# Chunk bounds by eight concurrent tiles over two banks, with a fence, in a statically ordered attention kernel

## The chip, the cores and the metric

The kernel runs on one core of a Trainium2 chip. The metric is the device time of one execution, in microseconds (us). Before the change it is 231.66 us, the median of three runs (231.29 to 232.64). "Engines" are PE (the matmul engine), PEld (its weight loads, which overlap PE: in the profile of before they are busy for 129.5 us beside PE's 214.9 in a span of 230.5), DVE (the vector engine), ACT (the scalar engine), POOL (GpSimd) and SP (which issues most DMAs: 153 of the 167 that the profile of before lists).

## The reference, cut to what matters

Four batches, eight heads, 768 positions, head dimension 64. Keys come in 24 chunks of 32. For each query an upper bound of its score with each chunk picks the six best chunks; attention runs only over those. A gated feed-forward block (gMLP) follows.

```python
k_min = np.min(k_chunks, axis=3)
k_max = np.max(k_chunks, axis=3)
ub = np.sum(np.maximum(q[:, :, :, None, :] * k_min[:, :, None, :, :],
                       q[:, :, :, None, :] * k_max[:, :, None, :, :]), axis=-1)
ub = np.where(causal, ub, -1000000000.0)
top_chunks = np.argsort(ub, axis=-1)[..., -top_k:]      # top_k = 6
...                                                     # masked softmax attention
h = gelu(x @ w_in); u, v = h[..., :512], h[..., 512:]   # (written out in the original)
v_s = np.einsum('ts,bsd->btd', w_sg, v_n) + b_sg[None, :, None]
return x + (u * v_s) @ w_out
```

Since max(q·lo, q·hi) = q·lo + max(q, 0)·(hi − lo) for hi ≥ lo, the bound is a sum of two matrix products: `W[0]` (the minima) with q, and `W[1]` (maxima minus minima) with `rT` = max(q, 0).

## The kernel before

Heads are worked on in 16 pairs (two heads on 128 partitions: head one on 0–63, head two on 64–127), and a *select* finds the chunks of two pairs at once, so there are eight selects. Every piece of work is handed to a small list scheduler written into the kernel. It is given an assumed cost for each operation and an urgency for each kind of work (a table found earlier by a search over the scheduler's own model of the time), and it fixes, before anything runs, in what order each engine executes. The program gives every engine its list as one stream, with waits on semaphores in it; at one such wait in the changed kernel PE idled 3.32 us and ran nothing else meanwhile (the timeline is below).

```python
# key side of a pair: W[w][:,0] = minima, W[w][:,1] = maxima, then the difference in place
P.op("dve", lambda d: d.tensor_tensor(W[w][:, 1, 0:NC], W[w][:, 1, 0:NC], W[w][:, 0, 0:NC],
                                      op=ALU.subtract), 0.18, port=True, reads=ws, writes=ws)
...
# query side of a pair: both heads at once, 128 partitions x 576 columns
P.op("dve", lambda d: d.tensor_scalar(rT[w % 2][:], qT[w][:, LO:S], 0.0, None, op0=ALU.max),
     0.47, port=True, reads=qk, writes=[("rT", w % 2)])
...
def select(pairs):
    u = sel_of(pairs[0])
    for hf in range(2):                       # two halves of 288 queries, one PSUM bank each
        t = ps_g.tile(t_slots(pairs[0]))
        n = NSEL // 2
        def ub(e, t=t, hf=hf):
            for m in range(2):                # first W·q, then (difference)·max(q, 0)
                for j in (0, 2, 1, 3):        # four heads: four 64x32 tiles of the array
                    w, lo = pairs[j % len(pairs)] % 4, 64 * (j // 2)
                    rhs = qT[w][lo:lo + 64, ...] if m == 0 else rT[w % 2][lo:lo + 64, ...]
                    r = e.matmul(t.ap()[32 * j:32 * j + 32, 0:n], W[w][lo:lo + 64, m, :], rhs,
                                 start=(m == 0), stop=(m == 1), tile_position=(lo, 32 * j))
            return r
        P.op("pe", ub, 1.0, mode="ub", reads=..., writes=[t], alloc=t)
        P.op("dve", lambda d, ...: d.transpose(U[u]..., t.ap()[:, 0:n]), dve(n, "ps"), ...)
    ...                                       # MAX8, comparison, transpose: the mask Dt
```

The number after each function (0.18, 0.47, 1.0) is the cost that the scheduler assumes. `SIDE = 6` says that the scores of the first six pairs are computed by `scores` (two matmuls on 64 rows each, the mask added by further matmuls), those of the others by `scores_one` (full rows, with the mask sent into the operand's spare rows by small DMAs).

The softmax here doesn't subtract the row's maximum and nothing guards it: scores larger than these inputs give would overflow.

Of the kernel before, what the change touches and what calls it, by code (L numbers as in the profile page):

```python
# [13 lines left out]
LAT = {"pe": 0.15, "act": 0.25, "dve": 0.12, "pool": 0.15, "sp": 0.05}  # L14
# [36 lines left out]
class Program:  # L51
# [11 lines left out]
    def op(self, eng, fn, cost, reads=(), writes=(), ps=(), alloc=None, dma=None, table=None,  # L63
           burst=None, prio=None, lane=0, bulk=False, port=False, mode="full"):
        o = Op()
# [8 lines left out]
        ps = tuple(ps) + ((alloc,) if alloc is not None else ())  # L74
# [32 lines left out]
    def schedule(self):  # L107
# [3 lines left out]
        alloc = {o.alloc: o for o in ops if o.alloc is not None}  # L111
# [28 lines left out]
        def slot_for(t, now):  # L140
            best = None
            for i, own in enumerate(t.cls.owner):
                if t.slots is not None and i not in t.slots:
                    continue
                at = 0.0 if own is None else (own.end if own.left == 0 else None)
                if at is not None and (best is None or at < best[0]):
                    best = (at, i)
            return best

# [4 lines left out]
        while n < len(ops):  # L154
            pick = None
            for e in ENGINES:
                cands = []
                for i in ready[e]:
                    o = ops[i]
                    t = max(rt[i], free[e])  # L160
                    if o.alloc is not None and o.alloc.slot is None:
                        s = slot_for(o.alloc, t)
                        if s is None:
                            continue
                        t = max(t, s[0])
# [19 lines left out]
            if o.alloc is not None and o.alloc.slot is None:  # L185
                at, s = slot_for(o.alloc, t)
                old = o.alloc.cls.owner[s]
                if old is not None:
                    for x in old.users:
                        o.deps.setdefault(x, False)  # L190
                o.alloc.slot = s
                o.alloc.cls.owner[s] = o.alloc
                o.alloc.users = []
# [191 lines left out]
    "load": [-109, -94, 104, 570, 740, 1507, 425, 238, 1704, 1924, 1908, 1646, -23, 1323, 1316, 193],  # L385
    "k": [-173, 1463, 2123, 1531, 780, 272, 805, 1232, 858, 260, 499, 2021, 1327, 265, 1662, 1220],
    "q": [153, 446, 1733, 1884, -53, 768, 1388, 1712, 646, 352, 1619, 149, 1838, -64, 891, 1804],
    "loadv": [1232, 1270, 290, 178, 1412, 1731, 1539, 1414, 2195, 1824, 620, 120, 73, 2088, 414, 668],
    "v": [1246, 1773, 342, 1920, 1326, 645, -200, -63, 1450, 33, 50, 561, 714, 486, 422, 351],
    "sel": [470, 1537, 1414, 781, 346, 556, 2087, -51, 3, 2114, 490, 1502, 1878, 798, 1690, -200],  # L390
    "sc": [-200, 1272, -200, 17, 1196, 1646, 1679, -197, -28, 1484, -90, 4, 1572, 21, 24, 44],
    "pv": [1443, 370, 1445, 454, 78, 2144, 1213, 76, 721, 1663, 938, 638, -147, 176, 1396, 952],
    "xt": [443, 2013, 57, 514, 469, 383, 911, -30, 421, 1131, 124, 1380, 1215, 390, 258, 433],
    "wsg": [-182],
    "hv": [497, 543, -154, 490],
    "hu": [2065, 884, 201, 728],
    "pt": [-96, 2026, 372, 745, 1924, 1969, 1334, 596],
    "out": [1127, 1638, 1477, 1797, 2040, 1893, 1475, -31],
# [3 lines left out]
def dve(n, src="sb", rate=1.0):  # L402
    return ((120 if src == "ps" else 58) + n / rate) / 960.0 + 0.04


def act(n):
    return 0.12 + n / 1200.0
# [10 lines left out]
def _kernel(nc, q, k, v, w_in, g_ln, w_sg, b_sg, w_out, out):  # L418
# [13 lines left out]
    SIDE = 6  # L432
    XDMA = 1
    WDMA = 0
    FIRST = 0
    ROWB = ()
# [27 lines left out]
    with contextlib.ExitStack() as ctx:  # L464
        def T(name, shape, dt):
            return ctx.enter_context(nc.sbuf_tensor(name, list(shape), dt))

        P = Program()
        ps_score = PsumClass([ctx.enter_context(nc.psum_tensor(f"PSC{i}", [128, 1024], F32)) for i in range(2)])
# [12 lines left out]
        bsgbc = T("bsgbc", [128, S], F32) if len(ROWB) < B else None  # L482
        if ROWB:
            glnbc = T("glnbc", [128, F], F32)
            bsg3 = T("bsg3", [128, S], BF16)
            bsgf = T("bsgf", [1, S], F32)
            onesB = T("onesB", [128, 128], BF16)
            nmr = T("nmr", [128, NT], F32)

# [6 lines left out]
        W = [T(f"W{i}", [128, 2, 32], F32) for i in range(4)]  # L496
# [21 lines left out]
        vsT = [T(f"vsT{i}", [128, TG], F32) for i in range(2)] if len(ROWB) < B else None  # L518
# [42 lines left out]
        def weights(when):  # L561
            for after, i in when:
# [15 lines left out]
                else:  # L578
                    if len(ROWB) < B:
                        P.op("sp", lambda s: s.dma_start(bsgbc[:], bass.AP(b_sg.tensor, 0, [[0, 128], [1, S]])),  # L580
                             2.3, reads=after, writes=["bsgbc"], dma="bsg")
                        P.op("sp", gln_load, 0.3, reads=after, writes=["glnT"], dma="gln")
                    if ROWB:
                        P.op("sp", lambda s: s.dma_start(bsgf[:], bass.AP(b_sg.tensor, 0, [[S, 1], [1, S]])), 0.2,
                             reads=after, writes=["bsgf"], dma="bsgf")
                        P.op("sp", lambda s: s.dma_start(glnbc[:], bass.AP(g_ln.tensor, 0, [[0, 128], [1, F]])), 1.6,
                             reads=after, writes=["glnbc"], dma="glnbc")
                        at("wsg", 0)
                        P.op("pool", lambda g: g.memset(bsg3[:], 0.0), 0.5, reads=after, writes=["bsg3"])
                        P.op("pool", lambda g: g.memset(onesB[:], 1.0), 0.2, reads=after, writes=["onesB"])  # L590
                        for r in (0, 32, 64):
                            P.op("pool", lambda g, r=r: g.tensor_copy(bsg3[r:r + 1, :], bsgf[:]), 0.8, lane=r + 1,
                                 reads=["bsgf", "bsg3"], writes=["bsg3"])
                            if r < 64:
                                P.op("pool", lambda g, r=r: g.tensor_tensor(bsgf[:], bsgf[:], bsg3[r:r + 1, :],
                                                                            op=ALU.subtract), 1.2, lane=r + 1,
                                     reads=["bsgf", "bsg3"], writes=["bsgf"])
# [18 lines left out]
        def kside(p):  # L616
            s, w = p % NQS, p % 4
            for hf in range(2):
# [13 lines left out]
                for kt_, rows, key in ([(KA, slice(0, 128), "KA")] if p < SIDE else  # L632
# [5 lines left out]
            P.op("dve", lambda d: d.tensor_tensor(W[w][:, 1, 0:NC], W[w][:, 1, 0:NC], W[w][:, 0, 0:NC],  # L638
                                                  op=ALU.subtract), 0.18, port=True, reads=ws, writes=ws)
# [4 lines left out]
        def qside(p):  # L644
            s, w = p % NQS, p % 4
            for hf in range(2):
                t = ps_g.tile(t_slots(p))

                def tr(e, t=t, hf=hf):
# [10 lines left out]
            P.op("dve", lambda d: d.tensor_scalar(rT[w % 2][:], qT[w][:, LO:S], 0.0, None, op0=ALU.max),  # L660
                 0.47, port=True, reads=qk, writes=[("rT", w % 2)])
# [14 lines left out]
        def sel_of(p):  # L676
            return p % 2 if p < FIRST else (p // 2 + FIRST // 2) % 2

        def select(pairs):
            u = sel_of(pairs[0])  # L680
            for hf in range(2):
                t = ps_g.tile(t_slots(pairs[0]))
                n = NSEL // 2

                def ub(e, t=t, hf=hf):
                    for m in range(2):
                        for j in (0, 2, 1, 3):
                            w, lo = pairs[j % len(pairs)] % 4, 64 * (j // 2)
                            rhs = qT[w][lo:lo + 64, LO + n * hf:LO + n * hf + n] if m == 0 else \
                                rT[w % 2][lo:lo + 64, n * hf:n * hf + n]  # L690
                            r = e.matmul(t.ap()[32 * j:32 * j + 32, 0:n], W[w][lo:lo + 64, m, :], rhs,  # L691
                                         start=(m == 0), stop=(m == 1), tile_position=(lo, 32 * j))
                    return r
                ws = [p % 4 for p in pairs]
                P.op("pe", ub, 1.0, mode="ub",
                     reads=[("qT", w, h_) for w in ws for h_ in range(2)] + [("rT", w % 2) for w in ws] +
                     [("W", w, m, h_) for w in ws for m in range(2) for h_ in range(2)],
                     writes=[t], alloc=t)
                P.op("dve", lambda d, t=t, hf=hf: d.transpose(
                    U[u][:].rearrange("p b c -> p (b c)")[:, n * hf:n * hf + n], t.ap()[:, 0:n]),  # L700
                    dve(n, "ps"), reads=[t], writes=[("U", u, hf)], ps=[t])
            P.op("dve", lambda d: d.memset(U[u][:, 0, TOP + 1:TOP + 2], -3.0e38), 0.07,
                 writes=[("U", u, 0)])

            def m8s(d):
                for b in range(NBLK):
                    r = d.max(m8[u][:, b, :], U[u][:, b, 0:max(8, b + TOP + 1)])
                return r
            P.op("dve", m8s, 1.47, reads=[("U", u, 0), ("U", u, 1)], writes=[("m8", u)])
# [3 lines left out]
                 0.75, port=True, reads=[("U", u, 0), ("U", u, 1), ("m8", u)], writes=[("Dn", u)])  # L713
# [214 lines left out]
        def moe_g(b):  # L928
            s = b % 2
            for tg in range(2):  # L930
                at("pt", 2 * b + tg)
                for fb in range(NF):
                    t = ps_g.tile((2, 3))

                    def pt(e, t=t, fb=fb, tg=tg):
                        if b in ROWB:
                            e.matmul(t.ap()[:, 0:TG], onesB[:], bsg3[:, TG * tg:TG * tg + TG], start=True, stop=False)
# [138 lines left out]
```

## Time and profile before

| | before |
|---|---|
| time, median | 231.66 us |
| span of the profiled run | 230.5 us |
| PE busy, DVE busy | 214.9 us (93%), 185.3 us (80%) |
| one half of the bounds (eight tile matmuls twice) | 1.11 us |
| `rT` and W difference on DVE, all 16 pairs | 12.4 us |
| first gelu table load after the start-up (the first feed-forward block begins) | 54.3 us |

From the profile's page of before: busy time by engine, the granted PE clock in 40 slices of the span, and the share of each engine in the chain of waits (the chain that ended last).

```profile
PE 214.9 (93%) x2267; PEld 129.5 (56%) x2280; DVE 185.3 (80%) x532; ACT 158.1 (69%) x244; POOL 90.9 (39%) x117
PEclk9999799999999999999999999999999999999999
PE 76%; DVE 10%; ACT 9%; DMA 2%; issue 1%
```

PE is almost always busy and makes up three quarters of the chain. A saving on PE looks like a saving of time; DVE has a fifth of its time free.

Stretches of before: window and length, then for each engine its busy time and (number of instructions), the granted clock, DMA share, GB/s.

```profile
core 0: us, PE busy (x) PEld busy (x) DVE busy (x) ACT busy (x) POOL busy (x), PEclk, DMA share, GB/s
20.00:40.00 20.00, 17.18 (x249) 9.96 (x250) 13.42 (x43) 16.25 (x26) 11.55 (x15) 0.91 1.03 206
40.00:60.00 20.00, 17.96 (x260) 11.56 (x260) 14.83 (x37) 17.14 (x28) 11.89 (x18) 1.00 1.15 232
60.00:80.00 20.00, 19.99 (x192) 11.65 (x191) 18.88 (x72) 13.28 (x22) 9.65 (x10) 1.00 0.96 186
80.00:100.00 20.00, 19.95 (x278) 13.46 (x278) 16.26 (x53) 17.75 (x29) 11.17 (x14) 1.00 1.01 212
```

Until 60 us PE has gaps; in the stretches after it is nearly full.

The DVE groups by form (line, engine, operation, output and input with shape, count; then busy us and mean ns of one; then idle time before them), and two rows of the timeline (start, length) with the matmuls of one half of the bounds.

```profile
L660 DVE TENSOR_SCALAR rT<-qT 128x576 f32<-128x576 f32 x16 | 8.5, 539 | 1.5 <-PE PSG L691 1.2 <-ACT qT L656 0.2
L638 DVE TENSOR_TENSOR W<-W 128x24 f32<-128x24 f32 x16 | 3.9, 247 | 0.1
```

```profile
125.09 0.69 PE L691 MATMUL PSG<-qT,W 64*32 64x288 f32 x8
125.60 0.67 PE L691 MATMUL PSG<-rT,W 64*32 64x288 f32 x8
```

One half runs from 125.09 to the next matmul at 126.20, so 1.11 us. In the single records the four tiles of a round start 6 to 7 ns apart and the rounds 0.24 us apart; each of the two terms shows two rounds of four.

### The profile page before, as it was taken

What the parts mean: (1) busy time and instruction counts of PE and PEld (TensorE: products, weight loads), DVE (VectorE), ACT (ScalarE), POOL (GpSimd) and SP (SyncE); (2) the same over time, 40 slices, a digit from 0 to 9 for tenths busy, and PEclk for the clock granted to TensorE, in tenths of its full rate; (3) what the DMA queues carried; (4) which work ended last, traced back from release to release, by engine and by line L of the source; (5) the groups of instructions that cost most, each with busy time, mean ns of one, the idle gap of its engine ahead of it and who ended that gap; (6) DMA issues with size and microseconds to landing.
All of it is one profiled execution on the core that took longest, in us unless ns stands there. A gap on an engine that the chain in (4) does not pass through costs nothing.

```text
span 230.5 us, 5838 instructions
## 1 busy us (share of the span) xinstructions
PE 214.9 (93%) x2267; PEld 129.5 (56%) x2280; DVE 185.3 (80%) x532; ACT 158.1 (69%) x244; POOL 90.9 (39%) x117
## 2 busy tenths in 40 slices
PE   7796989988999999999979999999999999999992
PEld 3453357654654665687745647875445976344440
DVE  3999296766899988698869889987897788777982
ACT  2455589996569588998999568899679676560000
POOL 8833385863546154747650305851022121020000
PEclk9999799999999999999999999999999999999999
DMA  8999899999959998867998010231003521102234
GB/s 157 215 216 197 191 221 224 242 239 236 203 113 226 208 178 204 246 103 144 180 263 151 0 30 0 56 74 49 1 0 119 174 34 37 45 0 91 94 135 184
DMA packets 90954, 31.59 MB, mean 137 GB/s; under 512 B 85456, under 2 KB 87216, under 8 KB 90928
## 3 DMA queue, kind: packets, MB, share of 16 engines
q1 hardware_dynamic: 88912, 28.47, 56.7%
q0 software_dynamic: 2016, 2.75, 7.2%
q8 instruction: 18, 0.29, 0.6%
q14 instruction: 8, 0.07, 0.1%
HBM read 24.77 MB, written 6.29 MB: 135 GB/s over the span
## 4 chain that ended last, share of the span: by engine, by line
PE 76%; DVE 10%; ACT 9%; DMA 2%; issue 1%
PE PSG L939 13%; PE PSG L918 10%; PE PSG L966 9%; PE PSC L789 9%; PE PSG L879 8%; PE PSG L691 8%; PE PSG L816 7%; ACT E L758 5%; DVE W L629 3%; PE PSG L623 3%; PE PSG L651 3%; PE PSC L740 2%; PE PSC L528 2%; DMA QA<-Dt 2%; PE PSC L746 1%; DVE rT L660 1%
## 5 line engine op out<-in xcount | busy, mean ns | idle before, releaser
L793 ACT ACTIVATE E<-PSC 128x1024 bf16<-128x1024 f32 (+1 forms) x60 | 52.1, 916 | 7.7 <-PE PSC L789 6.9
L629 DVE TENSOR_REDUCE W<-PSG 128x12 f32<-128x384 f32 x64 | 32.5, 548 | 6.9 <-PE PSG L623 6.7
L939 PE MATMUL PSG<-wsgT,vhat 128*128 128x384 bf16 x192 | 36.1, 326 | 0.2
L758 ACT ACTIVATE E<-PSC 128x1024 bf16<-128x1024 f32 (+1 forms) x36 | 31.3, 927 | 4.1 <-PE PSC L746 3.6
L797 POOL TENSOR_SCALAR_AFFINE_SELECT E<-E 128x768 bf16<-128x768 bf16 x20 | 18.4, 919 | 37.2 <-ACT E L793 37.0
L816 PE MATMUL PSG<-vx,E 128*128 128x65 bf16 x672 | 25.1, 194 | 0.8 <-ACT E L758 0.5
L816 PEld LDWEIGHTS PSG<-vx,E 128*128 128x128 bf16 x672 | 23.2, 98 | 3.1 <-DVE XS L826 0.9
L939 PEld LDWEIGHTS PSG<-wsgT,vhat 128*128 128x128 bf16 x192 | 17.2, 98 | 13.5 <-DVE vsT L952 1.9
L918 PE MATMUL PSG<-xT,winb 128*128 128x384 bf16 x128 | 24.0, 327 | 0.3 <-ACT uT L923 0.3
L879 PE MATMUL PSG<-winb,xT 128*128 128x512 bf16 x92 | 22.0, 379 | 1.9 <-ACT vgb L883 0.9
L952 DVE SCALAR_TENSOR_TENSOR vsT<-PSG,glnT,bsgbc 128x384 f32<-128x384 f32 x32 | 19.6, 614 | 4.1 <-PE PSG L939 3.6
L923 ACT ACTIVATE uT<-PSG 128x384 bf16<-128x384 f32 x32 | 15.7, 491 | 10.3 <-PE PSG L918 10.1
L966 PE MATMUL PSG<-woutb,uT 128*128 128x512 bf16 x88 | 22.1, 380 | 0.5
L634 ACT ACTIVATE KA<-PSG 64x384 bf16<-64x384 f32 (+1 forms) x32 | 15.5, 485 | 9.8 <-DVE W L629 9.8
L656 ACT ACTIVATE qT<-PSG 128x384 f32<-128x384 f32 x32 | 15.0, 495 | 8.8 <-PE PSG L651 8.6
L886 DVE BATCH_NORM_STATS2 stats<-vgb 128x6 f32<-128x512 f32 x24 | 16.2, 686 | 4.7 <-ACT vgb L883 4.7
L883 ACT ACTIVATE vgb<-PSG 128x512 f32<-128x512 f32 x24 | 14.1, 596 | 8.2 <-PE PSG L879 8.0
L972 DVE TENSOR_TENSOR osb<-PSG,XS 128x512 f32<-128x512 f32 x24 | 16.5, 686 | 4.0 <-PE PSG L966 3.3
L892 POOL TENSOR_TENSOR rstd<-rstd,neghalf 128x6 f32<-128x6 f32 x4 | 6.4, 1610 | 32.8 <-DVE rstd L890 32.7
L651 PE MATMUL PSG<-identF,qn 128*128 128x128 f32 x96 | 15.9, 282 | 2.9 <-ACT KA L634 1.7
L956 DVE TENSOR_TENSOR uT<-vsT,uT 128x384 bf16<-128x384 f32 x32 | 18.2, 580 | 0.5
L826 DVE TENSOR_TENSOR XS<-PSG,rden 128x384 bf16<-128x384 f32 x32 | 17.4, 549 | 0.5
(75 smaller groups left out, 375.0 us busy)
## 6 DMA issues: line engine op xcount, KB each, us to landing
kn<-in_k_dram SPq DMA_DIRECT2D x32, 192.0 KB, 4.1
qn<-in_q_dram SPq DMA_DIRECT2D x32, 192.0 KB, 3.6
vn<-in_v_dram SPq DMA_DIRECT2D x32, 192.0 KB, 4.2
out_dram<-osb SPq DMA_DIRECT2D x24, 256.0 KB, 2.0
winb<-in_moe_w_in_dram POOLq DMA_DIRECT2D x4, 256.0 KB, 5.0
vhat<-in_moe_w_sg_dram POOLq DMA_DIRECT2D x3, 192.0 KB, 5.7
uT<-in_moe_w_sg_dram POOLq DMA_DIRECT2D x3, 192.0 KB, 5.7
woutb<-in_moe_w_out_dram POOLq DMA_DIRECT2D x4, 128.0 KB, 4.9
```

What stands on the lines that cost most here:

```text
L629: P.op("dve", lambda d, t=t, m=m, op=op, hf=hf: d.tensor_reduce(W[w][:, m, 12 * hf:12 * hf + 12], t.ap()[:, 0:TG].rearrange("p (c x) -> p ...
L651: r = e.matmul(t.ap()[:, 128 * j:128 * j + 128], qn[s][:, 3 * hf + j].rearrange("p i d -> p (i d)"), identF[:], is_transpose=True)
L691: r = e.matmul(t.ap()[32 * j:32 * j + 32, 0:n], W[w][lo:lo + 64, m, :], rhs, start=(m == 0), stop=(m == 1), tile_position=(lo, 32 * j))
L758: P.op("act", lambda e, t=t, n=n, ev=ev: e.activation(ev, t.ap()[:, 0:1024].rearrange("p (i x) -> p i x", x=512)[:, :, 0:n], ACTF.Exp, sca ...
L789: r = e.matmul(t.ap()[:, o:o + n], kt_[rows, 128 * kb:128 * kb + 128], qt_[rows, q0:q0 + n], start=True, stop=True, skip_group_check=True)
L793: P.op("act", lambda e, t=t, c0=c0, c1=c1: e.activation(E[es][:, ETOT * i + c0:ETOT * i + c1], t.ap()[:, 0:c1 - c0], ACTF.Exp, scale=SCALE ...
L816: r = e.matmul(t.ap()[:, 65 * qb:65 * qb + 65], E[es][:, o:o + 128], vx[w][:, kb, i, :], start=(n == 0), stop=(kb == qb), skip_group_check ...
L879: r = e.matmul(t.ap()[:, 0:F], xT[s][:, dk, 128 * qt:128 * qt + 128], winb[:, dk, F:DFF], start=(dk == 0), stop=(dk == NDK - 1))
L918: r = e.matmul(t.ap()[:, 0:TG], winb[:, dk, 128 * fb:128 * fb + 128], xT[s][:, dk, TG * tg:TG * tg + TG], start=(dk == 0), stop=(dk == NDK ...
L939: r = e.matmul(t.ap()[:, 0:TG], vhat[s][:, sb, 128 * fb:128 * fb + 128], wsgT[:, sb, TG * tg:TG * tg + TG], start=(sb == 0 and b not in ROWB),
L952: P.op("dve", lambda d, t=t, fb=fb, tg=tg, vs=vs: d.scalar_tensor_tensor(vsT[vs][:], t.ap()[:, 0:TG], glnT[:, fb:fb + 1], bsgbc[:, TG * tg ...
L966: r = e.matmul(t.ap()[:, 0:DM], gT[s][:, fb, 128 * qt:128 * qt + 128], woutb[:, fb, :], start=(fb == 0), stop=(fb == NF - 1))
```

## The change

**Intent.** The traces write the largest weights of this kernel's matmuls as `128*128` and those of a bounds tile as `64*32`, an eighth of that, so four tiles together come to half of the largest. The change lets both halves of a select run at once: eight tiles over two PSUM banks. So that no two of the eight are given the same rows and columns (`tile_position`), the first half takes its W·q tiles at their usual rows while the second takes its difference·max(q, 0) tiles, with the operands of the two heads swapped between the lower and upper 64 partitions; then the roles swap. Since now tiles of different rows add to the same place in PSUM, a semaphore (the fence) holds the second step until the first is written. The swapped copies of `rT` and the W difference are made by DVE, in two operations of 64 partitions in place of one of 128. With it came `SIDE` 6 → 4 (pairs 4 and 5 no longer row-halved), a new urgency table from a new search, and new assumed costs.

```diff
-LAT = {"pe": 0.15, "act": 0.25, "dve": 0.12, "pool": 0.15, "sp": 0.05}
+LAT = {"pe": 0.15, "act": 0.31, "dve": 0.2, "pool": 0.15, "sp": 0.05}
 ... (the scheduler learns to give one operation two PSUM banks; URGENCY: all 169 numbers new)
-    SIDE = 6
+    SIDE = 4
 ...
-            P.op("dve", lambda d: d.tensor_tensor(W[w][:, 1, 0:NC], W[w][:, 1, 0:NC], W[w][:, 0, 0:NC],
-                                                  op=ALU.subtract), 0.18, port=True, reads=ws, writes=ws)
+            for a in (0, 64):
+                P.op("dve", lambda d, a=a: d.tensor_tensor(W[w][64 - a:128 - a, 2, 0:NC], W[w][a:a + 64, 1, 0:NC],
+                                                           W[w][a:a + 64, 0, 0:NC], op=ALU.subtract),
+                     0.1, port=True, reads=ws, writes=[("Wd", w, a)])
 ...
-            P.op("dve", lambda d: d.tensor_scalar(rT[w % 2][:], qT[w][:, LO:S], 0.0, None, op0=ALU.max),
-                 0.47, port=True, reads=qk, writes=[("rT", w % 2)])
+            for a in (0, 64):
+                P.op("dve", lambda d, a=a: d.tensor_scalar(rT[w % 2][64 - a:128 - a, :], qT[w][a:a + 64, LO:S], 0.0,
+                                                           None, op0=ALU.max),
+                     0.37, port=True, reads=qk, writes=[("rT", w % 2, a)])
 ...
+            def ub(e):
+                for step in range(2):
+                    if step:
+                        e.wait_ge(s_ub, fence[0])
+                    for hf in range(2):
+                        for j in (0, 2, 1, 3):
+                            w, a = pairs[j % 2] % 4, 64 * (j // 2)
+                            if hf == step:
+                                lhs, rhs, lo = W[w][a:a + 64, 0, :], qT[w][a:a + 64, LO + n * hf:LO + n * hf + n], a
+                            else:
+                                lo = 64 - a
+                                lhs, rhs = W[w][lo:lo + 64, 2, :], rT[w % 2][lo:lo + 64, n * hf:n * hf + n]
+                            r = e.matmul(half(hf)[32 * j:32 * j + 32, :], lhs, rhs, start=(step == 0),
+                                         stop=(step == 1), tile_position=(lo, 32 * j), skip_group_check=True)
+                            if step == 0:
+                                r.then_inc(s_ub, 1)
+                                fence[0] += 1
+                return r
 ...
+            P.op("pe", ub, 1.15, mode="ub", ...)
```

(Options of the kernel that no longer had a use were also removed; they changed nothing.) The cost formula of DVE was lowered by 0.095 us an operation, that of ACT by 0.055, and most single prices with them.

## The prediction

> **What bounds it now.** Span 230.5 us; the page's first part: PE 93%, DVE 80%, ACT 69%. The chain of waits is 76% PE. By stretches, PE is 98-100% busy from 60 to 200 us apart from 1.6 us near 105 us (mask DMA QA<-Dt, 3.8 us in the chain); before 60 us it is busy for 51.6, of which 8.5 us is warm-up filler. There ACT paces (30-50 us: 19.0 of 20 busy). So time = 19 us early idle and filler, 203 us real matmul slots (summed start to start), 4 us later gaps, 4 us tail.
>
> **What the change does.**
> - Chunk bounds. One half takes 1.11 us of PE now: four rounds of four 64x32 fp32 tiles, 0.242 us apart, plus 0.14 us of switching. Sixteen halves: 17.8 us (7.6% of the chain). Afterwards both halves share four rounds of eight tiles: 0.97 + 0.14, plus a fence. Fence, estimated: the last matmul lasts 0.40 us against a 0.24 pitch (0.16), matmul end to waiting engine 0.07 in the trace[...]. About 1.45 us a select instead of 2.22: 8 x 0.77 = 6.2 us off PE.
> - Pairs 4 and 5 move from row-halved to full scores: slots 2.44 us a pair against 2.83, 0.8 us off PE; 2 us more ACT copies (0.485 us each), four small mask DMAs more.
> - DVE pays: rT (0.45 us, 128 partitions) becomes two ops on 64 partitions, each with as many columns, so as long; likewise the W difference (0.18). 16 x 0.64 = 10 us more: about 196 us.
> - Order. Fillers rise from 25 to 36; three pairs, not two, are loaded before the first bounds (scores start some 1 us later); the first hv matmul has 46 us of PE slots before it, not 35.5, but also 13 us more ACT work, so it starts near 65-67 us instead of 54.4.
>
> **How much is critical.** Early idle and filler stays about 20 us: ACT-bound, so savings in the first two selects count little. After the first hv, PE slots fall from 168 to 150 us. 66 + 150 + 4 gaps + 4.3 tail = 224.5 us span, 225.5 timed. Against it: up to the third batch's hv DVE work grows from 131 to about 147 us, 93% of the time to there instead of 82%, so some PE waits on DVE (W, rT, vsT) appear. Each select also holds both transpose banks together.
>
> Predicted 225.3 us, 8 in 10 within 222 to 229.5. Faster by over 2% (below 227.1): 0.68; within: 0.28; slower: 0.04.
>
> **What the profile would show.** Bounds: 1.35 to 1.6 us a select, two groups of 16 matmul records with a gap of 0.2-0.4 us, tiles 6-7 ns apart; line total near 11.6 us. DVE busy 193-198 us, rT about 0.45 us x32. First gelu table load near 67 us. PE at 97%+ from 66 us to the last matmul. PE<-DVE waits of a few us.
>
> **What would make it wrong.** Eight tiles not running together (bounds stay near 2.2 us: about 230 us); a fence above 0.6 us; DVE pacing from 20 to 160 us (227-230); rT slowed by the partition shift or by contention with POOL (one took 1.10 us already); the new order hiding early idle better than I think (221).

Where the text is marked as cut, one term of the estimate of the fence is left out, because no trace or run here shows it. With it the sum came to the "about 1.45 us a select"; the terms that stand come to 1.34 us (0.97 + 0.14 + 0.16 + 0.07). The 6.2 us off PE and the 225.3 us predicted still include the cut term.

## The result, and the profile after

The changed kernel is correct and takes 246.2 us (median of four runs, 244.57 to 246.96) against 231.8 (four runs, 231.29 to 232.64) in the same rounds: a ratio of 1.061, with a 95% interval of 1.055 to 1.067. It is slower. A ratio here is always the mean time of one kernel's fast runs over that of the other kernel's fast runs of the same rounds, so it is not quite the ratio of the medians quoted.

| | before | after |
|---|---|---|
| span of the profiled run | 230.5 us | 245.2 us |
| PE busy | 214.9 us | 214.7 us |
| DVE busy | 185.3 us | 203.3 us |
| `rT` + W difference | 12.4 us | 28.8 us |
| bounds of one select on PE | 2 x 1.11 us | 1.68 us |
| first gelu table load after the start-up | 54.3 us | 80.7 us |
| mean granted PE clock | 0.993 | 0.969 |

The page of after: busy time, clock, chain.

```profile
PE 214.7 (88%) x2242; PEld 129.0 (53%) x2254; DVE 203.3 (83%) x564; ACT 161.3 (66%) x248; POOL 93.6 (38%) x119
PEclk9999869999689999999999999999999999999998
PE 50%; DVE 34%; ACT 6%; DMA 4%; issue 2%; SPq 2%; POOL 0%; DVEq 0%
```

DVE's share of the chain rises from 10 to 34%. PE's clock shows two dips where before had one. The PE busy time is no smaller although less work is done, because at half clock the same matmuls take longer: the rounds of the second select's bounds, at a granted clock of 0.50, start 0.48 us apart, those of the others 0.27.

The bounds do what they were meant to do. Timeline of after, one select; the brackets give PE's idle time and what ended it.

```profile
70.49 0.45 PE L693 MATMUL PSG<-qT,W 64*32 64x288 f32 x4
70.52 0.45 PE L693 MATMUL PSG<-rT,W 64*32 64x288 f32 x4
...
71.51 0.45 PE L693 MATMUL PSG<-rT,W 64*32 64x288 f32 x4 [0.30 <-PE PSG L693]
...
72.17 0.51 PE L796 MATMUL PSC<-QB,KB 128*128 128x128 bf16 x6
```

The second group of four starts 0.03 us after the first, so eight tiles do run together. The fence leaves PE idle for 0.30 us, and a select takes 72.17 − 70.49 = 1.68 us: at full clock 0.54 us saved on each of eight, 4.3 us in all. (The second select fell into a stretch at half clock and took 2.67 us.)

DVE's two groups, and the waits for `rT` (total us, times, longest), after and then before:

```profile
L651 DVE TENSOR_SCALAR rT<-qT 64x576 f32<-64x576 f32 x32 | 21.0, 655 | 1.2 <-ACT qT L646 0.5
L627 DVE TENSOR_TENSOR W<-W 64x24 f32<-64x24 f32 x32 | 7.8, 244 | 0.7
```

```profile
PE PSG L693 <- DVE rT L651: 4.3, 3, 3.3
PE PSG L691 <- DVE rT L660: 1.1, 1, 1.1
```

Half the partitions, twice the instructions, and each of them as long as the whole one or longer (655 ns against 539). Here is the longest wait of after, in the timeline:

```profile
25.47 1.10 DVE L651 TENSOR_SCALAR rT<-qT 64x576 f32<-64x576 f32 x1
26.50 0.36 DVE L627 TENSOR_TENSOR W<-W 64x24 f32<-64x24 f32 x2
26.77 2.53 DVE L651 TENSOR_SCALAR rT<-qT 64x576 f32<-64x576 f32 x3
27.01 1.98 POOL L772 TENSOR_SCALAR_AFFINE_SELECT E<-E 128x1024 bf16<-128x1024 bf16 x2 [0.75 <-ACT E L765]
29.35 0.70 PE L693 MATMUL PSG<-qT,W 64*32 64x288 f32 x4 [3.32 <-DVE rT L651]
```

Four half operations of two pairs stand in a row on DVE, while POOL works at the same time. PE, whose next entry is the second select, idles 3.32 us, and nothing later in its list runs in between.

Stretches of after:

```profile
core 0: us, PE busy (x) PEld busy (x) DVE busy (x) ACT busy (x) POOL busy (x), PEclk, DMA share, GB/s
20.00:40.00 20.00, 14.38 (x148) 6.99 (x148) 13.98 (x58) 10.47 (x18) 6.52 (x8) 0.83 1.00 181
40.00:60.00 20.00, 15.50 (x269) 10.09 (x267) 16.28 (x51) 17.56 (x28) 14.46 (x20) 1.00 0.97 185
60.00:80.00 20.00, 17.55 (x262) 13.66 (x264) 16.62 (x57) 13.95 (x21) 10.14 (x13) 0.83 0.71 151
80.00:100.00 20.00, 17.47 (x143) 10.18 (x146) 17.34 (x40) 17.89 (x33) 9.83 (x12) 1.00 0.94 185
```

Over these 80 us PE is busy 64.9 us against 75.1 before, and 40 of them have a mean clock of 0.83. The slow stretches last about 7 us each; this one is the second:

```profile
62.00:69.00 7.00, 6.69 (x77) 5.43 (x72) 5.03 (x11) 5.30 (x10) 3.86 (x6) 0.54 0.97 208
```

Before the tail of the span, the profile of after has two stretches at a granted clock of 0.50, of 6.83 us each (from 28.49 and from 62.63 us), and that of before has one, of 3.41 us (from 23.21 us). In a time as long as that one, 3.41 us, just before the two falls of after PE was busy for 0.95 and 1.72 us, and just before the one of before for 1.71. That does not make a rule: from 43.90 to 47.31 us of after PE was busy for only 1.57 us, and the clock stayed at 1.00. So what makes it fall is not shown here. Its cost comes on top of the idle time, since matmuls take longer while it lasts: e4 below, at a mean clock of 1.000, has 4.1 us less PE busy time for the same matmuls.

### The profile page after: what moved, and what is told of

It reads as the page before. It is cut to its first block, busy times and chain, and to the rows that moved or that the text cites. A ratio compares the mean times of both kernels' runs of the same rounds, so it can differ in the third digit from the quotient of the medians.

```text
span 245.2 us, 5828 instructions
## 1 busy us (share of the span) xinstructions
PE 214.7 (88%) x2242; PEld 129.0 (53%) x2254; DVE 203.3 (83%) x564; ACT 161.3 (66%) x248; POOL 93.6 (38%) x119
## 4 chain that ended last, share of the span: by engine, by line
PE 50%; DVE 34%; ACT 6%; DMA 4%; issue 2%; SPq 2%; POOL 0%; DVEq 0%
PE PSG L932 10%; PE PSC L796 8%; DVE W L617 7%; PE PSG L954 6%; DVE rT L651 6%; PE PSG L693 6%; PE PSG L913 5%; PE PSG L823 5%; PE PSG L886 5%; DVE XS L833 3%; DVE vhat L902 2%; DVE vsT L940 2%; DVE m L714 2%; DVE uT L944 2%; DMA vn<-in_v_dram 2%
## 5 line engine op out<-in xcount | busy, mean ns | idle before, releaser
L804 POOL TENSOR_SCALAR_AFFINE_SELECT E<-E 128x768 bf16<-128x768 bf16 x24 | 22.2, 926 | 48.4 <-ACT E L800 48.3
L932 PE MATMUL PSG<-wsgT,vhat 128*128 128x384 bf16 x192 | 35.6, 326 | 1.2 <-ACT uT L918 0.6
L823 PE MATMUL PSG<-vx,E 128*128 128x65 bf16 x672 | 26.2, 196 | 2.6 <-DVE vsT L940 1.1
L823 PEld LDWEIGHTS PSG<-vx,E 128*128 128x128 bf16 x672 | 24.1, 99 | 6.3 <-DVE vsT L940 1.8
L646 ACT ACTIVATE qT<-PSG 128x384 f32<-128x384 f32 x32 | 15.3, 500 | 12.5 <-PE PSG L641 12.5
L651 DVE TENSOR_SCALAR rT<-qT 64x576 f32<-64x576 f32 x32 | 21.0, 655 | 1.2 <-ACT qT L646 0.5
L944 DVE TENSOR_TENSOR uT<-vsT,uT 128x384 bf16<-128x384 f32 x32 | 20.4, 639 | 0.7
L796 PE MATMUL PSC<-QA,KA 88*128 88x128 bf16 (+2 forms) x168 | 19.4, 256 | 0.0
L665 POOL CAST vx<-vn 128x768 bf16<-128x768 f32 x16 | 14.5, 912 | 10.7 <-PE PSG L823 5.5
## 6 DMA issues: line engine op xcount, KB each, us to landing
kn<-in_k_dram SPq DMA_DIRECT2D x32, 192.0 KB, 3.6
qn<-in_q_dram SPq DMA_DIRECT2D x32, 192.0 KB, 3.6
vn<-in_v_dram SPq DMA_DIRECT2D x32, 192.0 KB, 3.6
vhat<-in_moe_w_sg_dram POOLq DMA_DIRECT2D x3, 192.0 KB, 4.5
uT<-in_moe_w_sg_dram POOLq DMA_DIRECT2D x3, 192.0 KB, 5.3
```

The lines of the kernel that those rows point to most:

```text
L651: P.op("dve", lambda d, a=a: d.tensor_scalar(rT[w % 2][64 - a:128 - a, :], qT[w][a:a + 64, LO:S], 0.0, None, op0=ALU.max), 0.37, port=True ...
L796: r = e.matmul(t.ap()[:, o:o + n], kt_[rows, 128 * kb:128 * kb + 128], qt_[rows, q0:q0 + n], start=True, stop=True, skip_group_check=True)
L823: r = e.matmul(t.ap()[:, 65 * qb:65 * qb + 65], E[es][:, o:o + 128], vx[w][:, kb, i, :], start=(n == 0), stop=(kb == qb), skip_group_check ...
L932: r = e.matmul(t.ap()[:, 0:TG], vhat[s][:, sb, 128 * fb:128 * fb + 128], wsgT[:, sb, TG * tg:TG * tg + TG], start=(sb == 0), stop=(sb == N ...
L944: P.op("dve", lambda d, fb=fb, tg=tg, vs=vs: d.tensor_tensor(gT[s][:, fb, TG * tg:TG * tg + TG], vsT[vs][:], uT[s][:, fb, TG * tg:TG * tg ...
```

## The experiments

What had to be told apart. **Theory 1**: the half operations on DVE cost the time. **Rival 2**: the bounds themselves are good or harmless, and the new order and row halving of fewer pairs cost it. **Rival 3**: eight tiles do not pay (the fence, or both banks held). Times are medians; the kernel before, run in the same rounds, had medians of 232.3 to 232.7 us. All runs used three rounds except e13 and e15, which used five.

### e1, e2, e3: one part of the change at a time, through the scheduler

e1 puts the new bounds and half operations into the kernel before and keeps its urgency table; e2 gives the changed kernel the old bounds and keeps its new table; e3 only sets `SIDE`:

```diff
 e1, on before:  + all of the diff of kside, qside, select and the scheduler (SIDE 6, old table)
 e2, on after:   - for a in (0, 64): ...half operations, ub with fence...   + the old lines
 e3, on before:  -    SIDE = 6   +    SIDE = 4
```

> The kernel before with the new bounds alone (eight tiles, fence, rT and W difference each as two swapped halves), its urgency table, latencies and six row-halved pairs kept. Theory D (the two swapped half-ops on DVE cost more than the eight tiles save): no faster than before, 232 to 242 us, DVE busy 198 to 204 us, bounds line about 14 us of PE slots. Theory O (the new order is what costs, the bounds by themselves pay): 225 to 230 us. Theory S (four row-halved pairs cost): 225 to 230 us too.

> The changed kernel with the old bounds put back (four tiles a half, one rT op and one W op on 128 partitions), new urgency, latencies, costs and four row-halved pairs kept. Theory D: 228 to 235 us, DVE busy near 186 us. Theory O: 242 us or more. Theory S: 242 us or more.

> The kernel before with four row-halved pairs instead of six, nothing else. Theory S: 238 us or more. Theories D and O: 229 to 234 us.

Measured: e1 267.3 us (ratio 1.138; two of its four runs were slow, 269.1 and 270.0 us at mean clocks of 0.947 and 0.945, and are left out of the ratio), e2 272.8 (1.171), e3 257.8 (1.109). Each is far worse than both kernels, whichever part it holds, so none of them tells the theories apart: three misses. They could have been foreseen: the scheduler's own model, which runs without a chip, puts the time of e1, e2 and e3 at 269.5, 260.6 and 262.5 us (before 237.4, after 231.7). What follows is about the method: the urgency table fits only the program that it was searched for. Change one operation, and the scheduler shuffles everything behind it, at 11 to 17% here. From here on the edits are made *inside* operations, so that the order on each engine stays fixed, or the order is searched again.

### e4: the changed kernel, its own order, whole-width operations

The first operation of each pair of halves does all 128 partitions in place; the second shrinks to a leftover of one or two columns. The swapped operands are then missing, so the result is wrong (relative error 0.55); the amount of work on every other engine is the same.

```diff
-   rT[w % 2][64 - a:128 - a, :], qT[w][a:a + 64, LO:S]
+   *((rT[w % 2][:, 2:], qT[w][:, LO + 2:S]) if a == 0 else (rT[w % 2][:, 0:2], qT[w][:, LO:LO + 2]))
```

(likewise the W difference: 24 columns, then one)

> The changed kernel with every instruction in the same order on each engine, but of each swapped pair the first op does all 128 partitions in place and the second only 2 columns (rT) or 1 (W): the results are wrong on purpose, the eight tiles and the fence stay. Theory D: 230 to 238 us, DVE busy near 190 us, the 3.3 us wait of the second select for rT near 29 us shrinks below 1.5 us. Theory O: 243 us or more. Theory S: 243 us or more.

Measured: 235.0 us, ratio 1.011 [1.004, 1.017]. That is 11.2 us under the changed kernel's median.

```profile
PE 210.6 (90%) x2254; PEld 127.4 (54%) x2254; DVE 192.7 (82%) x564; ACT 161.1 (69%) x248; POOL 92.7 (40%) x119
PEclk9999999999999999999999999999999999999999
```

DVE lost 10.6 us of busy time and the kernel 11.2 us of time. That is no proof that DVE time counts one for one, because the clock dips are gone too. Of the 11.2 us between the spans (245.2 and 234.0), 4.1 are PE busy time (214.7 and 210.6, the same matmuls at a mean clock of 0.969 and 1.000) and 7.1 are PE's idle time, of which the waits of the bounds for `rT` are 2.7 (4.3 and 1.6). The first gelu table load moves from 80.7 to 72.2 us, so 8.5 of the 11.2 us are won before it, in the early stretch where PE waits.

### e5: as e4, with the old four-tile bounds

> The changed kernel's instruction order with the in-place rT and W of the run before (one op on 128 partitions, one of 2 columns) and, inside the same place on PE, the old sequence of four tiles a half with no fence: right results. Beside the run with eight tiles in the same order (235.0 us) it tells what eight tiles are worth: 8 x (2.22 - 1.68) = 4.3 us of PE. Theory P (PE paces, the saving counts in full): 238.5 to 240 us. Theory L (most of it is lost in waits for DVE and ACT): 235 to 237 us.

```diff
-   for step in range(2):  ... wait_ge(s_ub, ...) ... eight tiles
+   for hf in range(2):
+       for m in range(2): ... four tiles, no fence
```

Measured: 238.6 us, ratio 1.026 [1.018, 1.034], correct, in the range of theory P. Against e4 (by the ratios, since they ran on different chips) the eight tiles are worth 3.6 us, of 4.3 us saved on PE. Rival 3 falls for this order.

### e6: eight tiles with no swap and no fence

The first half's four heads stay where they are. In the second half the heads on the lower rows take the columns of those on the upper rows and the other way round (`j ^ 2`), so the eight tiles have eight different places with each head on its own rows in both terms: no swapped copies, no fence. (In the kernel before, too, tiles of two row groups write different partitions of one PSUM bank; they start 6 to 7 ns apart, and the result is correct.) The mask of the second half then lies at other partitions, and each mask DMA becomes two. It is done for the six selects of pairs from `SIDE` on.

```diff
+   c = 32 * (j ^ 2 if hf == 1 and eight else j)
+   r = e.matmul(half(hf)[c:c + 32, :], W[w][a:a + 64, 2 * m, :], rhs, ..., tile_position=(a, c))
```

> The changed kernel's order, but the second half of the queries puts its heads into the other two column groups, so both terms of a head stay in one row group: eight tiles with no swap on DVE and no fence, for the six selects of fully scored pairs; their mask rows come by two DMAs a head instead of one; the first two selects use four tiles a half. Right results. Bounds about 1.1 us a select of six, 2.2 of two. Theory P: 231 to 233 us. Theory L: 234 to 236 us.

Measured: 235.1 us, ratio 1.012 [1.002, 1.021], correct; 3.5 us under e5 on the same chip. That is in the range of theory L: by the two sizes, six selects save PE an estimated 6 x 1.1 us, so about half of it came off the time. So the concurrency is to be had without any swapped copies. It still is not under the kernel before, in this order.

### e7: the kernel before, its own order, each operation split in two

The rival test of theory 1: only the splitting, nothing else of the change.

```diff
-   d.tensor_scalar(rT[w % 2][:], qT[w][:, LO:S], 0.0, None, op0=ALU.max)
+   [d.tensor_scalar(rT[w % 2][a:a + 64, :], qT[w][a:a + 64, LO:S], 0.0, None, op0=ALU.max) for a in (0, 64)][1]
```

> The kernel before, same order, each rT op and each W difference issued as two instructions on 64 partitions each, in place: right results, DVE busy up by 10 to 14 us, nothing else changed. Theory D (DVE has little slack in such a schedule, extra DVE work costs time nearly one for one): 238 to 244 us. If the schedule before has slack on DVE (80% busy): 232 to 235 us.

Measured: 245.4 us, ratio 1.055 [1.045, 1.065], correct. The split alone costs 13.0 us (245.35 − 232.37), in the old order with the old bounds. The same wait opens at the same place:

```profile
L661 DVE TENSOR_SCALAR rT<-qT 64x576 f32<-64x576 f32 x32 | 18.6, 580 | 0.8 <-PE PSG L693 0.4
```

```profile
28.24 1.18 PE L693 MATMUL PSG<-qT,W 64*32 64x288 f32 x8 [3.68 <-DVE rT L661]
```

### e8: the changed kernel with its halves not moved to other partitions

```diff
-   rT[w % 2][64 - a:128 - a, :], qT[w][a:a + 64, LO:S]
+   rT[w % 2][a:a + 64, :], qT[w][a:a + 64, LO:S]
```

Wrong (relative error 0.55).

> The changed kernel, same order, with the two half-ops of rT and W written to the partitions that they read instead of the other half: wrong results on purpose. If the number of columns is what costs: 244 to 248 us, as the changed kernel, rT mean near 0.65 us. If the shift of partitions is what costs: 234 to 238 us and rT mean below 0.5 us.

Measured: 245.8 us, ratio 1.056 [1.047, 1.065], `rT` 644 ns a half against 655. That the halves are moved to other partitions costs nothing that these times show (DVE is busy 201.9 us, 1.4 less); that there are two of them does. Whether it is their number or where each starts is the question of e9.

### e9: the kernel before, with whole operations issued twice

```diff
+   [d.tensor_scalar(x[:], qT[w][:, LO:S], 0.0, None, op0=ALU.max) for x in (rX[w % 2], rT[w % 2])][1]
```

As many extra instructions as e7, as many columns each, but all of 128 partitions and so all starting at the same partition (the first goes to a buffer that nobody reads; it holds bf16 in place of f32, and both take 0.45 us undisturbed).

> The kernel before, same order, each rT op and each W difference issued twice on all 128 partitions (the first copy into scratch nobody reads): as many DVE instructions as in the run with two halves of 64 partitions (245.4 us), but none starts at partition 64. In the traces a half-op takes 0.47 us (rT) and 0.19 us (W) from start to start, a whole one 0.37 and 0.10. Theory H (an op that starts at another partition loses its overlap with its neighbours, and that is a good part of the cost): extra DVE 16 x 0.47 = 7.5 us against 13.5, so 238 to 241 us. Theory C (only the number of ops counts): 244 to 247 us.

Measured: 239.9 us, ratio 1.034 [1.026, 1.042], correct: 7.2 us over before, against 13.0 for e7. The timeline shows why. Two operations back to back, undisturbed, first in e9, then in e7:

```profile
58.73 0.45 DVE L662 TENSOR_SCALAR rX<-qT 128x576 bf16<-128x576 f32 x1
59.09 0.45 DVE L662 TENSOR_SCALAR rT<-qT 128x576 f32<-128x576 f32 x1
```

```profile
60.55 0.56 DVE L848 COPY xT<-PSG 128x768 bf16<-128x768 bf16 x1
61.03 0.91 DVE L661 TENSOR_SCALAR rT<-qT 64x576 f32<-64x576 f32 x2
```

In e9 the second starts 0.36 us after the first, while that one is still running for 0.09. In e7 two take 0.91, so they do not overlap. Nor is it that operations of 64 partitions never overlap: the first half, which starts at partition 0 like the whole COPY in front of it, begins at 61.03, 0.08 us before that one ends at 61.11; the second, at partition 64, waits for the end of the first. Over all undisturbed pairs in the records the starts are 0.36 to 0.38 us apart for whole operations (0.09 to 0.10 for the W difference), and 0.45 to 0.47 (0.18 to 0.19) for the halves of e7 and of the changed kernel. Theory H (an operation that starts at another partition loses its overlap) stands. By these distances the price of the second start at partition 64 is about 0.1 us for each. Why it is held is not shown.

### e10, e11: single operations in the changed kernel's order

e10 removes the second half operation from DVE's list altogether and takes the four-tile bounds, so nothing of the idea is left: only the new order and `SIDE` 4. e11 adds the eight tiles of e6 to it.

```diff
 e10: + P.order["dve"] = [i for i in P.order["dve"] if i not in twin]     (second halves out; one 128-partition op)
 e11: + c = 32 * (j ^ 2 if hf == 1 and eight else j)                      (on e10)
```

> The changed kernel's order with the old bounds and truly one rT and one W op (the 2-column ops of the earlier runs are taken out): what the new order with four row-halved pairs is worth alone. Right results. If the new order is as good as the old: 231 to 233.5 us. If it is worse by itself: 234 to 238 us.

> As the run before it, but eight tiles with the second half's heads in the other column groups (no swap, no fence) for the six fully scored selects. Right results. Theory P: 3 to 4.5 us below the run before it, 230 to 233 us. Theory L: within 1.5 us of it.

Measured: e10 236.2 us, ratio 1.017 [1.008, 1.027]; e11 235.5, ratio 1.012 [1.001, 1.023]; both correct. The order and `SIDE` 4 alone cost about 4 us, which is rival 2's share. In e11 eight tiles gain only about 1 us and the intervals overlap, so whether they gain here is not settled. The leftover operations of e4 and e5 (DVE busy 192.0 us in e5, 185.3 in e10) may account for the 2 us between e10 and e5, which otherwise do the same; but these two ran on different chips and their intervals overlap, so the 2 us are not settled either.

### e12: the kernel before, its order, eight tiles in the last five selects

The two halves are merged, where the later of them stood in PE's list; tiles placed as in e6.

```diff
+   b_.fn = lambda e, ...: eight(e, (p0, p0 + 1), t0, t1)
+   P.order["pe"].remove(a_.idx)
```

> The kernel before, its own order and six row-halved pairs, with the two halves of the bounds merged at the place of the second and issued as eight tiles without swap and fence for the last five selects; two mask DMAs a head for them. Right results. Saves 5 x (2.22 - 1.11) = 5.5 us of PE. Theory P (PE paces there, 98 to 100% busy from 60 us on): 226.5 to 229 us. Theory L: 230 to 233 us.

Measured: 234.7 us, ratio 1.009 [0.998, 1.020], correct; the profiled run was slow (237.5 us at a mean clock of 0.985, the other three 233.0 to 234.7 at 0.991 to 0.999). An estimated 5 x 1.1 us of PE work is gone, and no time with it; theory P, which had it come off the time, falls, and even theory L's 230 to 233 us was too low. In that profile PE waits 3.1 us for loads of q and 2 us for the mask DMAs instead; since it is a slow run, these waits show where to look, not a cause.

### e13 to e16: the order searched again

The list scheduler can be asked what it believed: for the changed kernel it added up 175 us of DVE work, and the chip did 203. For the kernel before it added up 200, and the chip did 185: the old order had been booked with too much, the new one with too little. The half operations had been given the price of overlapped whole ones (0.37 and 0.1). They make up half of what is missing (booked 15.0 us, measured 28.8); the rest lies in the other operations, whose prices had been lowered too. (The scheduler does book DVE and POOL against each other: it starts an operation marked `port=True` only when the other engine's is over.) So one question remained: is the loss in the idea (more DVE work than any order can hide), or in the order, searched with prices that the chip does not honour? The four runs below use one search (simulated annealing over the scheduler's own model; by my own account, 3.5 million steps, and 1.2 million for e14, where a longer one found nothing better) and costs as measured here: 0.47 and 0.19 us for the halves, 0.5 for the split key copies; for the bounds 1.58 a select (e14, e16), two of 1.02 (e15), one of 1.03 (e13).

```diff
-                     0.37, port=True, reads=qk, writes=[("rT", w % 2, a)])
+                     0.47, port=True, reads=qk, writes=[("rT", w % 2, a)])
 ... 0.1 -> 0.19, 1.15 -> 1.58, and 169 new numbers in URGENCY; e16 also SIDE = 6
```

> The change itself, instruction for instruction (swapped half operands, fence, SIDE 4), but its order searched anew with the half operations costed as measured (0.47 and 0.19 us a half in place of 0.37 and 0.10, bounds 1.58 in place of 1.15, the split key copies 0.5). Model: 232.7 us. Theory C (the loss came from the wrong costs that the order was searched with): 235 to 239 us, at least 7 us under the changed kernel's 246, with DVE busy still 200 to 204. Theory D (the extra DVE work itself sets the time, whatever the order): 243 to 248 us.

> As e14 with SIDE 6 as in the kernel before, so the change's bounds alone with an order searched for them, the experiment that e1 was meant to be and could not. Model 232.1 us, 2.1 us over e15. Theory C: 235 to 239 us, 1 to 5 us over e15. Theory D: 243 to 248 us.

> Control for the search: the bounds of before (four tiles, two operations a select), SIDE 6, the same measured costs and the same search as e13. Model 230.0 us. If this search is as good as the one that gave the kernel before its table: 230 to 236 us. Above 238 the search is weaker and e13 and e14 can only be compared with e15, not with the kernel before.

> Eight concurrent tiles without swapped operands and without a fence (second half's heads in other column groups, one whole-width rT and W op, SIDE 6, so six selects of eight change at full and two stay four-tile), the order searched anew for just this program with operation costs measured in the earlier runs. The scheduler's own model gives it 226.9 us against 230.0 for e15 (same costs, same search length, old bounds). The model left out about 3 to 5 us that earlier runs took. Theory A (eight tiles are worth having once nothing is charged to DVE and the order fits): about 231.5 us, 3 us under e15, DVE busy 184 to 187 us. Theory B (saved PE time turns into other waits, mask DMA above all, as in e12): within 1 us of e15 or above it, with PE waiting on DMA for the masks or on DVE for over 4 us.

| run | what | model | measured (median) | ratio to before |
|---|---|---|---|---|
| e15 | old bounds, `SIDE` 6: the control | 230.0 | 236.8 us | 1.019 [1.014, 1.024] |
| e16 | the change's bounds, `SIDE` 6 | 231.9 | 235.6 us | 1.014 [1.009, 1.020] |
| e14 | the change's bounds, `SIDE` 4 | 232.7 | 242.0 us | 1.042 [1.037, 1.047] |
| e13 | eight tiles without swap or fence, `SIDE` 6 | 226.9 | 239.4 us | 1.031 [1.026, 1.035] |

All are correct. e16 comes nearest to an answer. It executes the same swapped halves and the same fence as the changed kernel:

```profile
PE 209.0 (89%) x2274; PEld 125.4 (53%) x2289; DVE 200.3 (85%) x564; ACT 158.0 (67%) x244; POOL 90.9 (39%) x117
PEclk9999999999999999999999999999999999999998
L651 DVE TENSOR_SCALAR rT<-qT 64x576 f32<-64x576 f32 x32 | 18.1, 566 | 2.6 <-PE PSG L693 1.9
PE PSG L693 <- DVE rT L651: 1.1, 2, 0.6
PE PSG L693 <- DVE W L627: 1.3, 1, 1.3
```

The control, e15:

```profile
PE 214.3 (91%) x2269; PEld 129.6 (55%) x2287; DVE 187.7 (80%) x532; ACT 157.5 (67%) x244; POOL 91.0 (39%) x117
```

DVE is busy 200.3 us, 12.6 more than in the control (187.7), and yet it is not slower than the control: the means of the fast runs are 235.7 and 236.5 us. The waits for `rT` fell from 4.3 us to 1.1 (with one of 1.3 for W) and the mean clock is 0.996. This is a balance, not a free ride: e16 also has 5.3 us less PE work than e15, so what it shows is that in a fitting order the DVE work costs no more than the tiles save. Theory D (the DVE work sets the time whatever the order) falls at `SIDE` 6. Theory C (the loss came from wrong prices in the search) is not shown by it: e16's time is in its range, but no run searched the change with the old prices, and with the new ones the scheduler still adds up only 181 us of DVE work for the 200 that the chip did. A new search may have been enough. For `SIDE` 4, the change itself, neither theory's range was met: e14 is 4 us under the changed kernel but above theory C's. There the bounds wait 0.3 us for `rT` and 2.8 for W, so `rT` alone is not what keeps it slow. Its search was the shorter one, so how much of the 6.3 us between e14 and e16 is `SIDE` and how much is the luck of the order stays open.

My search is not as good as the one that made the kernel before: the control is 4.4 us above it. So nothing here beats the kernel before, and e16 is compared with e15 alone.

e13 is a miss for theory A (its expectation also counts wrongly: with `SIDE` 6 five selects run as eight tiles and three as four). The model gave it the shortest time of all; on the chip it is 2.6 us over the control. The largest single wait:

```profile
117.63 2.41 SPq L829 DMA_TRANSPOSE xT<-XS  x1
...
122.54 3.57 PE L874 MATMUL PSG<-winb,xT 128*128 128x512 bf16 x8 [5.17 <-DMA xT<-XS]
```

A transposing DMA held its issuing queue for 2.41 us (the eleven of this run took 1.2 to 2.4 us each), where the model allows 0.5, PE idled 5.17 us for it, and the mean granted clock from 120 to 140 us was 0.83. The same kind of error, then, in another place: a price that the model has wrong. In the same trace PE also waits 4.4 us for masks on DVE, so theory B, which expected a loss to such waits, fits in part. It says nothing on eight tiles as such.

## Why the prediction was wrong

**Right.** Eight tiles run together. A select's bounds take one group of 16 matmuls, a gap, and another 16. `SIDE` 4 and the new order do bring more filler and a later first feed-forward block. DVE's work rises.

**Right in kind, small in effect.** The fence: predicted 1.45 us a select, measured 1.68, so the PE saving is 4.3 us in place of 6.2. The prediction's sum left 0.34 us for the fence, of which 0.23 (0.16 + 0.07) come from the trace of before and the rest was the term that is cut there; counted by starts it took about 0.48 (71.51 − 70.76 = 0.75 us from one round to the next, where 0.27 is usual). PE's idle gap in it is 0.30 us in the trace; what that gap is made of was not shown, and fewer increments were not tried.

**Wrong, first step: the size of DVE's work.** "16 x 0.64 = 10 us more: about 196 us." It was 18.0 us more, 203.3. `rT` and the W difference rose by 16.4 us. The single operation alone takes what was predicted: 454 ns where no POOL work overlaps it (452 for the whole one of before). But 18 of the 32 overlap POOL and then average 811 ns, up to 1.27 us; no half without such an overlap is longer than 0.46. (Before, 8 of 16 overlapped, at 626 ns, so the overlapped halves are no shorter than the overlapped whole ones.) Why they take longer beside POOL is not shown. The prediction listed contention with POOL among the risks and gave it no weight.

**Wrong, decisive step: how much of it lies on the critical path.** "Early idle and filler stays about 20 us" and, of DVE, that "some PE waits on DVE (W, rT, vsT) appear", put into 4 us of gaps with PE at 97% and more after 66 us. Of the 20.7 us by which the span missed (245.2 against 224.5), 14 to 15 are before the first gelu table load, which came at 80.7 us in place of 65 to 67, and 6 behind it. At fixed order the halves cost 11.7 us by their size (e4 to the changed kernel), and perhaps 2.1 more for the existence of a second instruction (e10 to e5, within the noise). The whole balance, each step being the difference of two ratios times 232.4 us (a median of before):

| step | us |
|---|---|
| before → e10: new order, `SIDE` 4, no new bounds | +4.0 |
| e10 → e5: a second, tiny operation each (within the noise) | +2.1 |
| e5 → e4: eight tiles and fence | −3.6 |
| e4 → after: the halves at full size | +11.7 |
| sum, which is after's own ratio of 1.061 | +14.1 |

The mechanism: the select stands in PE's list at a fixed place, and `rT` in DVE's. When DVE needs 0.47 us or, beside POOL, 0.81 for what the order had booked at 0.37, it and what stands behind it in DVE's list arrive late, PE runs nothing else meanwhile (3.32 us at the second select), and everything behind shifts. Twice in after a fall of the clock to 0.50 for 6.83 us followed; that the idle caused it is the author's reading, and not shown. In after, the idle time of PE that a wait for DVE ended was 12.5 us, against 6.7 in e4; `rT` for the bounds is 4.3 of it. DVE's free time lies elsewhere in this order and is not spent here. e7 shows it without the rest of the change, and e16 shows that another order can take the same DVE work: together with the eight tiles it is then no slower than its control. That the wrong prices are why the search found the bad order is likely, and not shown.

**What could have been seen.** The diff lists a cost of 0.37 us for an operation of 64 partitions whose whole-width predecessor the trace shows at 0.45. The prices of the order stood in the diff, and the sum of 175 us could be had without a chip. The prediction costed DVE itself and never asked what the search had believed.

## What to carry to other kernels

In a kernel whose order is frozen, work that exceeds its booked price can become a wait of another engine (3.32 us of PE here), even on an engine with idle time (DVE was 80% busy before); compare the costs in the scheduler, and their sum by engine, with measured durations before trusting an order found with them. Test parts of such a change with the order held fixed or searched anew for each, since a table tuned for one program cost 11 to 17% on its neighbours. Splitting one vector operation into two by partitions doubled its time here (twice 0.45 us in place of once), and before paying for swapped copies it is worth asking whether another placement of the tiles (e6) needs none.
